# One store of the tail, cut differently: two and a half chunks on 124 and 4 partitions in place of one chunk on 94 and 34

## The chip, the cores and the metric

The kernel runs on one core of one Trainium2 chip. The metric is the device time of one execution in microseconds. The five engines are TensorE (PE, with its weight loads shown as PEld), VectorE (DVE), ScalarE (ACT), GpSimd (POOL) and SyncE (SP). Transfers between HBM and SBUF run on 16 DMA engines that the core's queues share. A transfer that POOL issues is in queue q0 of the profile, one that ACT issues in q10, one that SP issues in q1; q8 and q14 are the queues that bring instructions.

## What is computed

Two stages. The first is cross-covariance attention over channels for four batches, the second a mixture of low-rank adapters on its result, for 25,600 rows of 256 columns:

```python
qn = q / (norm(q, axis=1) + 1e-06); kn = k / (norm(k, axis=1) + 1e-06)   # (4, 6400, 256)
a  = softmax(kn.transpose(0, 2, 1) @ qn / tau)                           # 256 x 256 a batch
x  = (v @ a).reshape(25600, 256)
logits = x @ w_gate                       # 8 experts, the two best are taken
w  = softmax over the two best
out = x + sum over the two of  w * (x @ A[e]) @ B[e]       # rank 16, float32 out
```

The output is 25,600 x 256 float32, 26.2 MB, and the three inputs are as large.

## The kernel before

A batch has 6,400 rows. Partition p holds rows 50p to 50p + 49 of the batch, so a batch is 50 chunks of 128 rows by 256 columns, and a chunk is one row of 1 KB (float32) on each of 128 partitions. Two chunks are a pair; the four batches have 100 pairs, 25 each. In HBM the rows of one partition lie behind each other, so that a store of n chunks is one contiguous run of n KB for each partition.

Loads of q, k and v go through POOL's queue, which casts them to bf16. PE accumulates the 256 x 256 product of a batch (L346), its column norms come from squares (L322, L331), then a short chain makes the softmax. For v, PE transposes the chunks (L507), computes the expert products (L639, L655) and the result of a pair (L672, L681) in PSUM, and ACT or DVE copies it to a staging tile `ys` (L691, L694). A planner in the kernel's Python simulates the engines and writes the order of all instructions out by hand; there is no other scheduler.

Stores. `BLOCKS` (L67) groups the pairs: eight blocks of ten pairs, then blocks of 5 + 5 and of 5 + 4 + 1. Each block has one `ys` tile, of which there are four (`YB`, L52). `send()` (L704) stores one group when all its pairs are in `ys`. Its queue is chosen in L718: POOL's for pairs 0 to 79 (`POOLED`), ACT's for the groups at 80, 85 and 90, SP's for the last two (pairs 95 to 98 and pair 99). A group that is named in `NARROW` (L63), here only that of pairs 80 to 84, is split: nine of its ten chunks go through ACT's queue over all 128 partitions (L722), and the tenth chunk goes through SP's queue as two transfers, partitions 0 to 93 and partitions 94 to 127 (L724). After these two, SP issues only the last two stores (L726) and then waits for all stores to land. The `ys` tile of pairs 80 to 89 is not used again, so no later instruction but the end of the kernel waits for these stores.

Of the kernel before, what the change touches and what calls it, by code (L numbers as in the profile page):

```python
# [16 lines left out]
def kernel(  # L17
# [16 lines left out]
    nc = tc.nc  # L34
    B, N, C = q.shape
    P = 128
# [25 lines left out]
    SPQ = 100  # L62
    NARROW = [80]  # L63
    CONST_SP = 0
    POOLED = range(0, 80)
    SEND_AT = [20, 34, 43, 56, 63]
    BLOCKS = [[10], [10], [10], [10], [10], [10], [10], [10], [5, 5], [5, 4, 1]]  # L67
# [23 lines left out]
    def run(e, us, *deps):  # L91
        clock[e] = max([clock[e]] + [d + (0.0 if e == "pe" else 0.05) for d in deps]) + us
        return clock[e] + (0.2 if e == "pe" else 0.0)
# [3 lines left out]
    def transfer(kind, us, start):  # L97
        x = {"left": us, "start": start, "done": None}
        wire[kind].append(x)
        return x  # L100
# [17 lines left out]
    def backlog():  # L118
        return sum(x["left"] for w in wire.values() for x in w)
# [128 lines left out]
    for n, (tile, src, us) in enumerate(consts):  # L248
        if n < CONST_SP:
            nc.sync.dma_start(tile, src)  # L250
        else:
            nc.gpsimd.dma_start(tile, src)
        transfer("load", us, run("pool", 0.55 if n >= CONST_SP else 0.0) + 1.5)

# [422 lines left out]
    def delta(p):  # L677
        r, x = unit_of[p]
        gr, y = stores[p], pr[p]["y"]
        for sc in range(2):  # L680
            nc.tensor.matmul(y[:, sc, :], r["gzT"][:, 2 * x + sc, :], ball_sb, start=False,  # L681
                             stop=(sc == 1), skip_group_check=True)
        blk = gr["blk"]
        if "ys" not in blk:
            blk["ys"] = y_pool.tile([P, 2 * YG, C], FP32, tag="ys", name="ys")
            ys_used.append(blk)
        w = 2 * (p - blk["f"])
        dst = blk["ys"][:, w:w + 2, :]
        t_end = run("pe", 0.215)
        if clock["dve"] + 1.0 < clock["act"]:  # L690
            nc.vector.tensor_copy(dst, y)  # L691
            end = run("dve", 0.69, t_end)
        else:
            nc.scalar.copy(dst, y)  # L694
            end = run("act", 0.58, t_end)
        pr[p]["y_end"] = gr["y_end"] = end
        if p == gr["f"] + gr["n"] - 1:
            unsent.append(gr)
            if p >= LATE:
                send()  # L700
# [3 lines left out]
    def send():  # L704

        gr = unsent.pop(0)
        f, n, w = gr["f"], 2 * gr["n"], 2 * (gr["f"] - gr["blk"]["f"])
        b, c = f // NPAIR, 2 * (f % NPAIR)
        src = gr["blk"]["ys"][:, w:w + n, :]
        if c + n <= NC:  # L710
            dst = out_v[b, :, c:c + n, :]
        else:

            h = n // 2
            assert c + h == NC
            dst = bass.AP(out.tensor, (b * N + c) * C, [[NC * C, P], [(N - c) * C, 2], [1, h * C]])
            src = src.rearrange("p (x c) d -> p x (c d)", x=2)
        eng = nc.sync if f >= NPT - GRP or f >= SPQ else nc.gpsimd if f in POOLED else nc.scalar  # L718
        if f in NARROW:

            m = n - 1
            eng.dma_start(dst[:, 0:m, :], src[:, 0:m, :])  # L722
            for lo, hi in ((0, 94), (94, P)):
                nc.sync.dma_start(dst[lo:hi, m:n, :], src[lo:hi, m:n, :])  # L724
        else:
            eng.dma_start(dst, src)  # L726
        if eng is nc.gpsimd:
            gr["sent"] = transfer("load", n * CHUNK + 0.05, run("pool", 0.55, gr["y_end"]) + 1.5)
        else:
            gr["sent"] = transfer("store", n * CHUNK + 0.05, run("act", 0.06 if eng is nc.scalar else 0.0, gr["y_end"]) + 3.0)  # L730
# [21 lines left out]
    def last_v():  # L752
        return there("v", B - 1, NC - 1)

    while nd < NPT:
# [5 lines left out]

        while unsent and ((nd >= SEND_AT[unsent[0]["f"] // 10] if unsent[0]["f"] in POOLED and unsent[0]["f"] < 50 else backlog() < BACKLOG) or not loads and not wire["load"] and now > last_v() + 0.0 or
                          sum("sent" not in b["all"][-1] for b in ys_used) > YB - 1):
            send()
# [4 lines left out]
        n = 4 if starved else 1  # L769
# [51 lines left out]
        if nt < NU:  # L821
            r = units[nt]
            ok = nt < VTB or ny >= units[nt - VTB]["p"] + units[nt - VTB]["n"]
            p = r["p"] % NPAIR
# [10 lines left out]
        if gi["b"] < B:  # L835
            b, c = gi["b"], gi["c"]
# [65 lines left out]
    while unsent:  # L902
        send()
# [35 lines left out]
```

## Time and profile before

| | |
|---|---|
| median of 3 runs | 253.91 us (253.84 to 253.92) |
| profiled execution, its own time | 253.94 us |
| span of its trace | 252.1 us |
| outside the span | 1.8 us |
| PE busy | 209.5 us (83%) |
| ACT busy | 167.1 us (66%) |
| DVE busy | 164.6 us (65%) |
| mean busy share of the DMA engines, last 33 us of the span | see the stretches in the prediction |

The page and the views give shares of the 16 DMA engines together. A share of 1.00 means that all 16 work, 0.50 that eight do. A packet is booked with its whole duration to the stretch in which it starts, and successive packets of an engine overlap a little, so that shares can come out slightly above 1. A packet of a store is one contiguous run of one partition; each DMA engine closes its part of a transfer with a 4-byte packet, which the views count among those "under 512 B". The counts "under 2 KB" and "under 8 KB" include the smaller ones. None of the views names the DMA engine of a packet.

### The profile page before, as it was taken

What the parts mean: (1) busy time and instruction counts of PE and PEld (TensorE: products, weight loads), DVE (VectorE), ACT (ScalarE), POOL (GpSimd) and SP (SyncE); (2) the same over time, 40 slices, a digit from 0 to 9 for tenths busy, and PEclk for the clock granted to TensorE, in tenths of its full rate; (3) what the DMA queues carried; (4) which work ended last, traced back from release to release, by engine and by line L of the source; (5) the groups of instructions that cost most, each with busy time, mean ns of one, the idle gap of its engine ahead of it and who ended that gap; (6) DMA issues with size and microseconds to landing.
All of it is one profiled execution on the core that took longest, in us unless ns stands there. A gap on an engine that the chain in (4) does not pass through costs nothing.

```text
span 252.1 us, 6727 instructions
## 1 busy us (share of the span) xinstructions
PE 209.5 (83%) x2870; PEld 185.5 (74%) x2870; DVE 164.6 (65%) x420; ACT 167.1 (66%) x256; POOL 31.0 (12%) x63
## 2 busy tenths in 40 slices
PE   0468088579799999999998999898999999999930
PEld 0345067457688999999997888797988898999820
DVE  1541646774478788887957689769587696777410
ACT  2654065773659678999656598956698768576730
POOL 8111102102201200111301101030020000010000
PEclk9995759968979999999999999999999999999995
DMA  7999999999999999999999999999999999999995
GB/s 219 213 214 214 236 220 214 213 214 213 214 217 220 214 215 217 211 216 218 214 404 235 217 213 219 256 413 383 222 213 222 257 376 310 422 431 412 424 428 209
DMA packets 8898, 66.76 MB, mean 265 GB/s; under 512 B 980, under 2 KB 1124, under 8 KB 5412
## 3 DMA queue, kind: packets, MB, share of 16 engines
q0 software_dynamic: 7872, 60.04, 94.2%
q10 hardware_dynamic: 432, 3.80, 3.6%
q1 hardware_dynamic: 564, 2.49, 2.6%
q8 instruction: 22, 0.36, 0.5%
q14 instruction: 8, 0.07, 0.1%
HBM read 78.91 MB, written 26.21 MB: 417 GB/s over the span
## 4 chain that ended last, share of the span: by engine, by line
DMA 41%; PE 40%; issue 5%; DVE 5%; ACT 2%; POOL 2%; POOLq 0%; DVEq 0%
DMA vt<-in_v_dram 13%; PE y_ps L672 11%; DMA qt<-in_q_dram 10%; DMA kt<-in_k_dram 10%; DMA wst<-in_moe_w_gate_dram 9%; PE acc L346 9%; PE y_ps L681 5%; PE vT_ps L507 5%; PE zg L639 4%; PE zg L655 2%; PE nrm L361 2%; DVE s L331 2%; PE lp L535 1%; ACT sq L322 1%; ACT ys L694 1%
## 5 line engine op out<-in xcount | busy, mean ns | idle before, releaser
L346 PE MATMUL acc<-qt,kt 128*128 128x256 bf16 x400 | 61.2, 309 | 3.9 <-DMA kt<-in_k_dram 3.8
L694 ACT COPY ys<-y_ps 128x512 f32<-128x512 f32 x92 | 52.1, 586 | 15.9 <-PE y_ps L681 14.7
L672 PE MATMUL y_ps<-a_bf,vT 128*128 128x256 bf16 x400 | 59.1, 272 | 1.6 <-ACT ys L694 1.5
L346 PEld LDWEIGHTS <-kt 128*128 128x128 bf16 x400 | 41.9, 110 | 13.2 <-DMA kt<-in_k_dram 4.5
L322 ACT ACTIVATE sq<-qt 128x1024 bf16<-128x1024 bf16 (+1 forms) x42 | 40.6, 1013 | 15.3 <-DVE s L331 13.0
L322 ACT ACTIVATE sq<-kt 128x1024 bf16<-128x1024 bf16 (+1 forms) x43 | 42.2, 1013 | 12.8 <-DVE s L331 7.6
L331 DVE TENSOR_TENSOR s<-sq 128x512 bf16<-128x512 bf16 x104 | 38.6, 408 | 9.1 <-PE nrm L361 5.9
L672 PEld LDWEIGHTS <-vT 128*128 128x128 bf16 x400 | 36.2, 98 | 5.5 <-issue 2.3
L643 DVE TENSOR_TENSOR gz<-zg,e 128x512 bf16<-128x512 f32 (+1 forms) x52 | 33.9, 665 | 9.4 <-PE zg L639 9.1
L361 PE MATMUL nrm<-ones_bf,s 128*128 128x1 bf16 x398 | 21.1, 165 | 21.8 <-DVE s L331 19.8
L361 PEld LDWEIGHTS <-s 128*128 128x128 bf16 x398 | 18.6, 98 | 25.8 <-DVE s L331 22.8
L681 PE MATMUL y_ps<-ball_sb,gzT 128*128 128x256 bf16 x200 | 36.2, 272 | 0.1
L507 PE MATMUL vT_ps<-ident,vt 128*128 128x128 bf16 x400 | 29.9, 219 | 2.2 <-DMA vt<-in_v_dram 1.0
L517 DVE COPY vT<-vT_ps 128x1024 bf16<-128x1024 bf16 (+1 forms) x36 | 23.5, 658 | 12.2 <-PE vT_ps L507 11.8
L639 PE MATMUL zg<-wa_sb,vT 128*128 128x128 bf16 x400 | 29.5, 219 | 0.0
L507 PEld LDWEIGHTS <-vt 128*128 128x128 bf16 x400 | 24.9, 98 | 3.8 <-issue 1.5
L639 PEld LDWEIGHTS <-vT 128*128 128x128 bf16 x400 | 25.1, 98 | 0.5
L514 ACT COPY vT<-vT_ps 128x1024 bf16<-128x1024 bf16 x16 | 16.1, 1014 | 11.7 <-PE vT_ps L507 11.7
L209 POOL DMA_DIRECT2D qt<-in_q_dram x16 | 8.6, 538 | 96.2 <-ACT sq L322 34.1
L655 PE MATMUL zg<-ident,gz 128*128 128x128 bf16 x200 | 19.3, 219 | 0.5 <-DVE gz L643 0.5
L663 DVE COPY gzT<-zg 128x512 bf16<-128x512 bf16 (+1 forms) x33 | 13.3, 408 | 9.1 <-PE zg L655 9.0
L681 PEld LDWEIGHTS <-gzT 128*128 128x128 bf16 x200 | 17.5, 97 | 2.3 <-DVE gzT L663 0.3
(71 smaller groups left out, 169.5 us busy)
## 6 DMA issues: line engine op xcount, KB each, us to landing
out_dram<-ys POOLq DMA_DIRECT2D x8, 2560.0 KB, 36.3
qt<-in_q_dram POOLq DMA_DIRECT2D x12, 768.0 KB, 22.3
kt<-in_k_dram POOLq DMA_DIRECT2D x12, 768.0 KB, 25.4
vt<-in_v_dram POOLq DMA_DIRECT2D x8, 1024.0 KB, 29.9
vt<-in_v_dram POOLq DMA_DIRECT2D x4, 1152.0 KB, 27.0
kt<-in_k_dram POOLq DMA_DIRECT2D x4, 896.0 KB, 22.1
qt<-in_q_dram POOLq DMA_DIRECT2D x3, 896.0 KB, 20.1
out_dram<-ys ACTq DMA_DIRECT2D x2, 1280.0 KB, 11.6
```

Source lines behind the costliest of these rows:

```text
L322: nc.scalar.activation(sq, x, ACT.Square)
L331: nc.vector.tensor_tensor(out=s2, in0=sq[:, 0:n, :], in1=sq[:, n:2 * n, :], op=OP.add)
L346: nc.tensor.matmul(acc[b][:, ic, :], tk[:, o, ic * P:(ic + 1) * P], tq[:, o, :], start=(c == 0 and ic == 0), stop=(c == NC - 1), skip_grou ...
L361: nc.tensor.matmul(nrm[b][:, j:j + 1], s2[:, x, ic * P:(ic + 1) * P], ones_bf[:, 0:1], start=(i == 0 and x == 0 and ic == 0), stop=(i >= l ...
L507: nc.tensor.matmul(pt[:, ic, sc, :], vt[:, o, ic * P:(ic + 1) * P], ident, is_transpose=True, start=(i == 0), stop=(i == 2 * nch - 1))
L517: nc.vector.tensor_copy(vT, pt)
L639: nc.tensor.matmul(z[:, sc, :], r["vT"][:, ic, sc, :], st[b]["wa"][:, ic, E:E + ER], start=(sc == 0 and ic == 0), stop=(sc == nch - 1 and ...
L643: nc.vector.tensor_tensor(out=gz.rearrange("p c (e r) -> p c e r", e=E), in0=z.rearrange("p c (e r) -> p c e r", e=E), in1=gr["gate"][:, r ...
L655: nc.tensor.matmul(gt[:, sc, :], r["gz"][:, sc, :], ident, is_transpose=True, start=(sc == 0), stop=(sc == nch - 1))
L672: nc.tensor.matmul(y[:, sc, :], r["vT"][:, ic, 2 * x + sc, :], st[r["b"]]["a"][:, ic, :], start=(sc == 0 and ic == 0), stop=False, skip_gr ...
L681: nc.tensor.matmul(y[:, sc, :], r["gzT"][:, 2 * x + sc, :], ball_sb, start=False, stop=(sc == 1), skip_group_check=True)
L694: nc.scalar.copy(dst, y)
```

## The change

The group of pairs 80 to 84 is cut at another place. Before, the last of its ten chunks (256 columns, 1 KB a partition) went through SP, cut into 94 and 34 partitions. After, the chunks of a partition are taken as one row of 2,560 columns, of which the last 640 (two and a half chunks, 2.5 KB a partition) go through SP, cut into 124 and 4 partitions. The part that ACT's queue stores over 128 partitions shrinks from nine chunks (9 KB a partition) to seven and a half (7.5 KB). The number of transfers, their queues and their order among the other instructions of each engine stay as they were.

```diff
     SPQ = 100
     NARROW = [80]
     CONST_SP = 0
+    NCOL = 640
+    NROW = 124
...
         if f in NARROW:
 
-            m = n - 1
-            eng.dma_start(dst[:, 0:m, :], src[:, 0:m, :])
-            for lo, hi in ((0, 94), (94, P)):
-                nc.sync.dma_start(dst[lo:hi, m:n, :], src[lo:hi, m:n, :])
+            dst, src = dst.rearrange("p c d -> p (c d)"), src.rearrange("p c d -> p (c d)")
+            m = n * C - NCOL
+            eng.dma_start(dst[:, 0:m], src[:, 0:m])
+            for lo, hi in ((0, NROW), (NROW, P)):
+                nc.sync.dma_start(dst[lo:hi, m:], src[lo:hi, m:])
         else:
             eng.dma_start(dst, src)
```

## The prediction

> **What bounds the kernel now.** I read the last stretches first, because the change touches only a store that is issued at 228 us. Columns: stretch, its length, busy time of PE, PEld, DVE, ACT and POOL with instruction counts, granted clock, share of the 16 DMA engines, GB/s.
>
> ```profile
> 240.00:244.00 4.00, 2.00 (x19) 1.35 (x16) 0.72 (x3) 1.75 (x3) 0.00 (x0) 1.00 1.01 424
> 244.00:248.00 4.00, 0.00 (x0) 0.00 (x0) 0.00 (x0) 0.00 (x0) 0.00 (x0) 0.81 0.92 385
> 248.00:250.80 2.80, 0.00 (x0) 0.00 (x0) 0.00 (x0) 0.00 (x0) 0.00 (x0) 0.50 0.49 200
> 250.80:252.10 1.30, 0.00 (x0) 0.00 (x0) 0.00 (x0) 0.00 (x0) 0.00 (x0) 0.50 0.00 0
> ```
>
> From 244 us on no engine computes; the kernel only drains stores, and the last packet ends at 250.8. The drain is uneven: a share of 0.92, then 0.49. The idle part is 0.08 x 4 x 16 + 0.51 x 2.8 x 16 = 28 engine-us, so a perfectly even drain would end 28 / 16 = 1.75 us earlier. That is the most that any recutting of stores can win.
>
> Next, who drains when. The last store (pair 99) gives every DMA engine eight packets of 2 KB (256 KB over 128 partitions), as the last of its list. Their number is "under 8 KB" minus "under 2 KB", in 240 to 247.0, 247 to 248, 248 to 249.2 and 249.2 to 250.9 us:
>
> ```profile
> DMA packets 441, 2.91 MB, mean 415 GB/s; under 512 B 47, under 2 KB 126, under 8 KB 158
> ...
> DMA packets 48, 0.33 MB, mean 333 GB/s; under 512 B 1, under 2 KB 12, under 8 KB 12
> ...
> DMA packets 77, 0.36 MB, mean 299 GB/s; under 512 B 12, under 2 KB 12, under 8 KB 42
> ...
> DMA packets 93, 0.20 MB, mean 118 GB/s; under 512 B 19, under 2 KB 19, under 8 KB 85
> ```
>
> That is 32, 0, 30 and 66 packets: four engines are through by 247.0, none ends in the next microsecond, between three and four end by 249.2, and some eight to nine between 249.2 and 250.8.
>
> Where the narrow chunk is, in the views of 220 to 253 us, 231.8 to 243.4 us and 232 to 247.46 us:
>
> ```profile
> q1 hardware_dynamic: 420, 1.44, 10.7%
> ...
> DMA packets 599, 4.90 MB, mean 422 GB/s; under 512 B 46, under 2 KB 115, under 8 KB 115
> q10 hardware_dynamic: 311, 2.80, 57.3%
> q1 hardware_dynamic: 69, 0.07, 1.7%
> ...
> DMA packets 870, 6.45 MB, mean 417 GB/s; under 512 B 72, under 2 KB 200, under 8 KB 232
> ```
>
> SP's 420 packets are 128 of 1 KB, 128 of 8 KB, 128 of 2 KB and 36 closing ones. The two full stores close on 16 engines each, which leaves 36 - 32 = 4 for the two narrow ones: two engines each. Of 94 and 34 the only divisors up to 16 are 1 and 2, while 128 has 16, so a transfer seems to use as many engines as divide its partitions. I take both narrow transfers to sit on the same two engines: 47 + 17 = 64 packets of 1 KB on each. By 247.46 us all 128 (200 - 72) have started, the last after 247.4. Behind it the same queue of that engine still holds eight packets of 8 KB and eight of 2 KB, 0.082 MB. The view of 247.46 to 250.8 us gives their price:
>
> ```profile
> q1 hardware_dynamic: 174, 0.63, 46.2%
> ```
>
> 0.462 x 16 x 3.34 us for 0.63 MB is 39 us a MB, so 3.2 us: the later narrow engine ends near 250.65, a hair before the slowest engine at 250.8.
>
> **The change, part by part.** Durations of one packet. 1 KB: 0.017 x 16 x 11.6 us / 69 = 46 ns. 9 KB: q10 in the same view, 0.573 x 16 x 11.6 us / 2.80 MB = 38 us a MB, so 350 ns, and 292 ns for 7.5 KB. 2 KB from the view of 250.4 to 250.9 us, where only the last store runs:
>
> ```profile
> DMA packets 13, 0.02 MB, mean 41 GB/s; under 512 B 3, under 2 KB 3, under 8 KB 13
> q1 hardware_dynamic: 13, 0.02, 10.8%
> ```
>
> 0.108 x 16 x 0.5 us over ten packets is 86 ns. The trace has no packet of 2.5 KB. From below its bytes at 38 us a MB are 97 ns, from above two and a half packets of 1 KB are 115 ns; a line through 46 and 86 ns gives 106 ns, and I take 100, nearer to the long packets, because the bookings overlap (shares of 1.01).
>
> Which engines: 124 and 4 partitions have 4 as their largest common divisor with 16, so by the pattern above each of the new transfers uses four engines, 31 + 1 = 32 packets each. No view shows which; I take the old two to be among them, as the transfers come from the same queue and as a count that does not fill 16 is likely dealt from the same start. The Trainium skill, "DMA: Bandwidth & Descriptors", section "Why a DMA increments its semaphore by 16 and not by 1", says the same of the count and adds that SP's and ACT's transfers take the lowest-numbered engines; the counts of 36 and 420 agree with the first part, no row here can show the second. By it, too, the old two are among the four.
>
> - All 16 engines: eight packets of 7.5 KB in place of 9 KB, 8 x (350 - 292) = 0.47 us less.
> - The two engines that had 1 KB packets: 32 x 100 - 64 x 46 = +0.26 us, less 0.47, so -0.2 us; with the ends 97 and 115 ns it is -0.3 to +0.3.
> - Two engines that had none: 32 x 100 = 3.2 us (3.1 to 3.7) less 0.47, so +2.7 us (2.6 to 3.2).
> - Issue. The three instructions stay where they are:
>
> ```profile
> 228.07 1.37 SPq L724 DMA_DIRECT2D out_dram<-ys  x2
> 229.22 0.38 ACTq L722 DMA_DIRECT2D out_dram<-ys  x1
> 241.75 1.48 SPq L726 DMA_DIRECT2D out_dram<-ys  x2
> SPq L934 <- DMA out_dram<-ys: 7.6, 6, 3.1
> ```
>
> If SP's two took 1.3 times as long (124 partitions against 94), SP would still be free 12 us before its next store at 241.75, and only the end waits for them; cost 0. Without that cover it would be the 0.4 us. ACT's issue stays one instruction; cost 0.
>
> The order of the queues does not matter: each engine has work without a gap to its end, so its end moves by the change of its own sum.
>
> **The sum.** Everything hangs on where the two new engines stood. If they are two of the four that were through by 247.0, they end at 249.6 to 249.8 and are covered by the others. The slowest engines go from 250.8 to 250.3, the later narrow engine from 250.65 to about 250.5 (250.3 to 250.95). The end is then near 250.55, 0.25 us earlier: 253.94 - 0.25 = 253.7 for the profiled execution, which is 0.03 above the median of the runs, so 253.7 again.
>
> Why the four should be among the early. Take the narrow packets away, 64 x 46 ns = 2.9 us, and the two narrow engines would have ended by 247.8, ahead of the gap in which none ends. So six of 16 engines are early without them, and both narrow ones belong to the six; by chance that happens in 6 x 5 of 16 x 15 cases, 1 in 8. Extra work that only some engines carry, such as the instruction fetches
>
> ```profile
> q8 instruction: 22, 0.36, 0.5%
> ```
>
> (0.005 x 16 x 252 us / 22 = 0.9 us each), is then more likely dealt out in blocks of neighbours, and the two neighbours of spared engines are likelier to be spared than 4 x 3 of 14 x 13.
>
> **The rivals.**
>
> *One of the two new engines is a late one of the middle group* (slower). For it: ten of the other 14 engines were not through by 247.0, and the views name no engine. Three or so end between 248.0 and 249.2. Put +2.7 us on one that ended at 248.7 and it ends at 251.4, on one at 249.2 and it ends at 251.9: 0.6 to 1.1 us after 250.8, so 254.5 to 255.0, most likely 254.5, since a spared neighbour with a little extra work is the likeliest of these. It decides as soon as one new engine ended later than 250.8 - 2.7 = 248.1. Against it: the argument of neighbours.
>
> *A new engine is one of the slowest* (slower). Ended 249.2 to 250.8, it now ends at 251.9 to 253.5: 255.0 to 256.6. For it speaks only their number, eight or nine; against it that the first two engines were both early.
>
> *The cut does not use four engines.* If 124 and 4 partitions spread over all 16, each engine would get eight packets of 2.5 KB, 0.8 us, less 0.47 us: the slowest ends 0.3 us later, the narrow ones much earlier, 254.2. If they stayed on two, these would get 64 x 100 ns and end 3 us later; the divisors speak against both. [...]
>
> **How the numbers follow.** Changes within 0.2%, 0.51 us, are about what a measurement of this kernel cannot tell from none: 253.40 to 254.42. All new engines early: 0.41, at 253.7, with its bounds 253.4 to 254.0 (0.03 of it below 253.40, as the relief of the slowest engines by 0.47 us is nearly all that could be won). A middle one: 0.33, at 254.5 to 255.0, of which 0.05 falls inside. A slowest one: 0.18. Spread over 16, or stayed on two: 0.08, nearly all of it the former and inside. So faster 0.03, same 0.38 + 0.05 + 0.08 = 0.51, slower 0.28 + 0.18 = 0.46. The range goes from 253.3 to 255.0 and leaves out the 0.18. The likeliest case alone has 253.4 to 254.0.
>
> **What would show it.** In the profile after, SP's queue has 424 packets in place of 420 (36 + 4 closing ones) if four engines are used, 448 if 16. The last 2 KB packets tell the rest: in the likeliest case 16 of them are written by 247.0 in place of 32, as two of the four early engines are left, and the last is written by 250.6. If the end comes after 251.2 with a share of one engine (0.06) for half a microsecond or more before it, one new engine was late; with two engines (0.12) beyond 252, a slow pair. If the wide part did not shrink each engine's list by 0.47 us, the step with 7.5 KB is wrong; if the packets of 2.5 KB take over 115 ns, the narrow engines set the end.

## The result, and the profile after

The changed kernel takes 254.59 us (median of 10 runs, 254.46 to 254.65), the kernel before 253.91 us (median of 10, 253.83 to 253.98): 0.68 us more, a ratio of 1.0027 with an interval of 1.0017 to 1.0036. The forecast was 253.7; what came is the first rival, a new engine out of the middle group, which was priced at 254.5.

The profiled execution took 254.47 us, with a span of 252.7 us. Its last stretches, in the columns of the stretches before (DMA share and GB/s at the end of the row):

```profile
240.00:244.00 4.00, 2.34 (x23) 1.64 (x20) 1.06 (x3) 1.97 (x4) 0.00 (x0) 1.00 1.00 421
244.00:248.00 4.00, 0.00 (x0) 0.00 (x0) 0.00 (x0) 0.00 (x0) 0.00 (x0) 0.78 0.92 383
248.00:250.80 2.80, 0.00 (x0) 0.00 (x0) 0.00 (x0) 0.00 (x0) 0.00 (x0) 0.50 0.50 205
250.80:251.50 0.70, 0.00 (x0) 0.00 (x0) 0.00 (x0) 0.00 (x0) 0.00 (x0) 0.50 0.06 23
251.50:252.70 1.20, 0.00 (x0) 0.00 (x0) 0.00 (x0) 0.00 (x0) 0.00 (x0) 0.50 0.00 0
```

The DMA shares of the first three rows are those of before within 0.01. The fourth is new: a share of 0.06 for 0.7 us is one engine of 16 (1 / 16 = 0.0625), writing alone where before nothing was written. This is the sign that the prediction named for one late new engine.

The packets of the same execution, in 240 to 247.0, 247 to 248, 248 to 249.2, 249.2 to 250.9 and 250.9 to 251.5 us, and SP's queue in 220 to 254 us:

```profile
DMA packets 397, 2.90 MB, mean 414 GB/s; under 512 B 43, under 2 KB 43, under 8 KB 122
...
DMA packets 50, 0.32 MB, mean 321 GB/s; under 512 B 8, under 2 KB 8, under 8 KB 14
...
DMA packets 88, 0.38 MB, mean 314 GB/s; under 512 B 13, under 2 KB 13, under 8 KB 52
...
DMA packets 87, 0.20 MB, mean 118 GB/s; under 512 B 16, under 2 KB 16, under 8 KB 78
...
DMA packets 7, 0.01 MB, mean 20 GB/s; under 512 B 1, under 2 KB 1, under 8 KB 7
...
q1 hardware_dynamic: 424, 1.64, 11.8%
```

SP's packets went from 420 to 424, so the two new transfers close on four engines each. "Under 8 KB" minus "under 2 KB" now counts packets of 2.5 KB and of 2 KB together: 79, 6, 39, 62 and 6. The records give 64 of the 128 packets of 2.5 KB before 240 and nine after 247.0, so that 55 of the 79 are of 2.5 KB, and 79 - 55 = 24 of the 2 KB packets were written by 247.0: three engines were through, where before there were four and where the likeliest case had two. The last row is the late engine: six packets of 2 KB and their closing packet.

The computation also ended 0.35 us later in this execution. The last copy of ACT, before and then after:

```profile
242.03 0.58 ACT ys L694
```

```profile
242.38 0.59 ACT ys L696
```

That could explain half of the loss, if the last stores were late for all engines. The 15 other engines say no: from 250.9 us on none of them works, and before none worked after 250.8. And in the runs below this copy comes earlier or later without the time following it: at 241.73 us with five engines, 1.72 us slower than before, and at 242.68 us with 384 columns, which is not slower.

**The end of each engine.** No view names the engine of a packet, but the records carry a packet's queue, size, start and duration, and on an engine the next packet begins where the last one ended. So they can be strung into 16 lists. This is a reconstruction, and single links may be wrong; the ends, where few engines are left, are safe. The last packet of each list, in us of the span:

```
kernel   engines with narrow packets         the early ones left     all others end by
before   249.44, 250.57                      4: 246.54 to 246.91     250.80
after    249.35, 249.67, 250.82, 251.46      3: 246.22 to 246.66     250.21
```

In before, the other ten end at 248.68, 249.12, 249.19 and, seven of them, from 250.05 to 250.80. I call the engines by the order in which narrow transfers of two, three, four or five engines reach them: first and second (those of before), third, fourth, fifth. The third is one of the four early ones. The fourth ended at 248.68 before and at 251.46 after, 2.78 us later; the end of the trace moved with it (251.46 - 250.80 = 0.66 us, of 0.68 us in the time).

### The profile page after: what moved, and what is told of

It reads as the page before. It is cut to its first block, busy times and chain, and to the rows that moved or that the text cites. A ratio compares the mean times of both kernels' runs of the same rounds, so it can differ in the third digit from the quotient of the medians.

```text
span 252.7 us, 6727 instructions
## 1 busy us (share of the span) xinstructions
PE 209.3 (83%) x2870; PEld 185.5 (73%) x2870; DVE 164.8 (65%) x420; ACT 167.1 (66%) x256; POOL 31.0 (12%) x63
## 4 chain that ended last, share of the span: by engine, by line
DMA 43%; PE 39%; issue 5%; DVE 5%; ACT 2%; POOL 2%; DVEq 0%; POOLq 0%
DMA vt<-in_v_dram 14%; PE y_ps L674 10%; DMA qt<-in_q_dram 10%; DMA kt<-in_k_dram 10%; PE acc L348 9%; DMA wst<-in_moe_w_gate_dram 9%; PE y_ps L683 5%; PE zg L641 4%; PE vT_ps L509 4%; PE zg L657 2%; PE lp L537 2%; DVE s L333 1%; ACT sq L324 1%; PE nrm L363 1%; ACT ys L696 1%
## 5 line engine op out<-in xcount | busy, mean ns | idle before, releaser
L519 DVE COPY vT<-vT_ps 128x1024 bf16<-128x1024 bf16 (+1 forms) x36 | 23.6, 660 | 12.4 <-PE vT_ps L509 11.8
```

The costliest lines, as they stand in the source:

```text
L519: nc.vector.tensor_copy(vT, pt)
```

## The experiments

The theory was that the time is set by the last engine, and that each engine's end moves by the packets it gains less what the wide store sheds; the third engine would be early and the fourth middle. The rivals in the expectations put the loss down to the larger narrow packets, the number of engines in a narrow transfer, or the later computation. The edits are against the kernel after. Each run has the kernel before on the same chip beside it: 253.72 us for 64 and 64 partitions, 256 columns, three transfers and seven engines; 253.91 for three engines in two transfers, five engines and the first try with memsets; 253.86 for 384 columns and the second try.

**The same bytes on all 16 engines.** The 640 columns are cut into 64 and 64 partitions.

```diff
-            for lo, hi in ((0, NROW), (NROW, P)):
+            for lo, hi in ((0, 64), (64, 128)):
```

> The same 640 columns through SP's queue, but cut into 64 and 64 partitions, which both use all 16 DMA engines: nothing is piled on a few engines any more. Theory T (after the change one of the four engines, a middle one that ended near 248.7 us before, got 3.2 us more and ends last): every engine has 8 x 7.5 KB and 8 x 2.5 KB in place of 8 x 9 KB, +0.33 us against a kernel before whose slowest engines end at 250.8, so 254.2 to 254.3; six engines are through by 247.5 (48 packets of 2 KB). Rival P (packets of 2.5 KB cost far more than 100 ns): as slow as the changed kernel or slower, 254.6 and above. Rival C (the computation ends later with the change, the drain only follows): 254.6, last ACT copy later than 242.0.

253.95 us, 0.23 more than before, ratio 1.001 (1.0 to 1.0019). SP's queue and the last stretches:

```profile
q1 hardware_dynamic: 448, 1.64, 11.1%
...
248.00:250.80 2.80, 0.00 (x0) 0.00 (x0) 0.00 (x0) 0.00 (x0) 0.00 (x0) 0.50 0.47 193
250.80:251.50 0.70, 0.00 (x0) 0.00 (x0) 0.00 (x0) 0.00 (x0) 0.00 (x0) 0.50 0.02 9
```

448 is 64 closing packets, 32 of them for the two narrow transfers: 16 engines each. Bytes, columns, packet size and wide store are those of after, only the engines differ, and 0.45 of the 0.68 us is gone. What is left is the difference of eight packets of 2.5 KB (102 ns each in the records) against 8 x 57 ns from the wide packets, +0.36 us on every engine; the last one ends at 251.05, 0.25 us later than before.

**Four engines, a small piece.** The cut at 124 stays, the piece is one chunk.

```diff
-    NCOL = 640
+    NCOL = 256
```

> The cut at 124 and 4 partitions alone, with the 256 columns of the kernel before: four engines get 32 packets of 1 KB (1.36 us) in place of 64 on two. Theory T: the middle engine ends near 248.7 + 1.36 = 250.05, the slowest engines keep their 250.8, so 253.9 as before. Rival F (four engines as such are slow, through the issue of 124 rows or the third and fourth engine's rate): over 254.2.

253.61 us, 0.11 less, ratio 0.9995 (0.9985 to 1.0004): no change that can be told. The same four engines do no harm by themselves. The fourth now gets 32 packets of 46 ns, which would put it at 248.68 + 1.47 = 250.15; its list ends at 250.01.

**Four engines, one and a half chunks.**

```diff
-    NCOL = 640
+    NCOL = 384
```

> 124 and 4 partitions by 384 columns, between the 256 and the 640 tried. Theory T: 32 packets of 1.5 KB are 1.95 us, so the fourth engine ends at 248.65 - 0.15 + 1.95 = 250.45, the slowest at 250.65: 0.1 to 0.2 us faster than the kernel before. If the loss grew with the width in proportion (from -0.11 at 256 to +0.68 at 640 columns): 0.15 us slower.

253.69 us, 0.17 less, ratio 0.9994 (0.9985 to 1.0002). SP's issue of the last two stores and the last stretches:

```profile
242.40 1.69 SPq L729 DMA_DIRECT2D out_dram<-ys  x2
...
248.00:250.80 2.80, 0.00 (x0) 0.00 (x0) 0.00 (x0) 0.00 (x0) 0.00 (x0) 0.50 0.50 203
250.80:251.50 0.70, 0.00 (x0) 0.00 (x0) 0.00 (x0) 0.00 (x0) 0.00 (x0) 0.50 0.00 0
```

The last stores are issued at 242.40 us, 0.3 us later than in the kernel after (242.10 us, below), and the row of one engine alone has gone. The fourth engine ends at 250.66, by now just the last (the next is at 250.57), but still ahead of the 250.80 of before; somewhere between 384 and 640 columns it begins to cost time. Its step of 0.80 us from 250.66 to 251.46 is that between the two profiled executions (253.66 and 254.47 us); the medians, on two chips, are 0.90 us apart. Against before, the last packet ends 0.14 us earlier, of the 0.17 us in the time.

**Three engines, in three transfers.** 123, 3 and 2 partitions, 432 columns, so that each of three engines gets about as much time as each of four did.

```diff
-    NCOL = 640
+    NCOL = 432
...
-            for lo, hi in ((0, NROW), (NROW, P)):
+            for lo, hi in ((0, 123), (123, 126), (126, 128)):
```

> 123, 3 and 2 partitions by 432 columns: by divisors three engines with 42 packets of 1.7 KB (68 ns each, 2.9 us), one more on the first two. It tells whether the late engine is the third or the fourth. If the fourth: the narrow engines end near 250.6, the slowest at 250.8 - 0.21 = 250.6, so 253.7. If the third: it ends at 248.7 - 0.2 + 2.85 = 251.3, so 254.4 to 254.5. If the transfers don't go by divisors, SP's queue has more than 128 x 3 + 39 = 423 packets of the last 33 us.

254.02 us, 0.30 more, ratio 1.0019 (1.0009 to 1.0028). Neither number. The last packet ends at 250.46, 0.34 us earlier than before, as the theory wants, but the execution takes 252.2 - 250.46 = 1.7 us to its end. What SP waits for at its closing line, in this kernel, and then the head of its page:

```profile
SPq L937 <- DMA out_dram<-ys: 7.5, 2, 7.2
```

```profile
span 252.2 us, 6729 instructions
```

Before, the same wait had six parts with 3.1 us as the longest; now one part of 7.2 us takes nearly all. SP checks its semaphores one after another, and here it stood at that of the last store first. Seven checks followed once the store had landed. The times of these events in the trace, in us:

```
before     250.302  250.615  251.243
k3_432     250.873  250.934  250.999  251.060  251.119  251.181  251.240  251.302
```

Seven steps of 61 ns are 0.43 us. The third narrow transfer is the ninth that SP and ACT issue through their queues, and I read the new order as a semaphore used twice; the order is shown, that cause is argued.

**Three engines, in two transfers.** The same columns, cut into 123 and 5 partitions. The 5 go one each to five engines.

```diff
-    NCOL = 640
-    NROW = 124
+    NCOL = 432
+    NROW = 123
```

> As the cut for three engines with 432 columns, but with two transfers (123 and 5 partitions) in place of three. In the run with three transfers the last packet ended 0.34 us earlier than in the kernel before, yet the time was 0.3 us longer: SP's closing sequence then checked the last store's semaphore first and seven others after it, 62 ns each. Theory T (third engine early, fourth late): without that the gain shows, 0.1 to 0.25 us faster than the kernel before. Rival (three engines are no better balanced and the time follows the number of engines): 0.2 to 0.3 us slower, as with three transfers.

253.72 us, 0.19 less, ratio 0.9993 (0.9984 to 1.0003).

```profile
SPq L937 <- DMA out_dram<-ys: 6.3, 4, 3.6
```

The wait is in four parts again, and the 0.49 us to the run before agree with the 0.43. This is the run that places the engines: three get 42 packets of 72 ns, +2.8 us after the wide store's relief, as much as each of four in the kernel after (32 x 103 ns - 0.46 = 2.8), and nothing is lost. So the third engine was early, and the loss of the kernel after is that of the fourth.

**Five engines.** 544 columns on 125 and 3 partitions: 25 packets of 88 ns on each of five engines.

```diff
-    NCOL = 640
-    NROW = 124
+    NCOL = 544
+    NROW = 125
```

> 125 and 3 partitions by 544 columns: five engines with 25 packets of 2.1 KB (2.1 us), 26 on the first three; every engine is relieved by 0.34 us. It places the fifth engine. Early: the middle engine ends at 248.6 - 0.34 + 2.1 = 250.4, the slowest at 250.45, so 0.3 us faster than the kernel before. Slow (249.7 to 250.8 before): it ends at 251.5 to 252.6, so 0.7 to 1.8 us slower.

255.63 us, 1.72 more, ratio 1.007 (1.0056 to 1.0083).

```profile
248.00:250.80 2.80, 0.00 (x0) 0.00 (x0) 0.00 (x0) 0.00 (x0) 0.00 (x0) 0.50 0.46 186
250.80:251.50 0.70, 0.00 (x0) 0.00 (x0) 0.00 (x0) 0.00 (x0) 0.00 (x0) 0.50 0.06 23
251.50:253.70 2.20, 0.00 (x0) 0.00 (x0) 0.00 (x0) 0.00 (x0) 0.00 (x0) 0.50 0.03 11
```

Again one engine alone (0.06), now until 252.50. Each of the five gains 25 x 88 ns less 8 x 42 ns, 1.87 us, so this one stood at 250.63 without it: one of the slowest seven. Another of the five ends at 250.38, near the 248.68 + 1.87 = 250.55 of the fourth. The fifth engine is the second rival of the prediction, met one engine later.

**Seven engines.** 800 columns, 119, 7 and 2 partitions.

```diff
-    NCOL = 640
+    NCOL = 800
...
-            for lo, hi in ((0, NROW), (NROW, P)):
+            for lo, hi in ((0, 119), (119, 126), (126, 128)):
```

> 119, 7 and 2 partitions by 800 columns: by divisors seven engines with 18 packets of 3.1 KB (2.2 us), 19 on the first two. Theory T with the early engines as neighbours (all three that are early in both traces are the fifth to seventh): the slowest engines go from 250.8 to 250.15, the middle one to 248.7 - 0.65 + 2.2 = 250.25, so 253.3 to 253.4, faster than both. If one of the fifth to seventh is a slow engine it ends near 252.3, so 255.4 or so.

255.71 us, 1.99 more, ratio 1.0079 (1.0062 to 1.0095).

```profile
q1 hardware_dynamic: 432, 1.72, 11.7%
```

432 packets are 16 closing ones for the narrow transfers, 7 + 7 + 2. The last packet ends at 252.14, 1.34 us later than before; SP's seven checks behind the last store are there again (252.613 to 253.042 us), and with their 0.43 us that is 1.77 of the 1.99 us. Engines in a block of neighbours are not spared alike.

**What makes the fourth engine later, first try.** Both kernels, before and after, get 400 short memsets of DVE spread over the first stage, so that DVE fetches more instructions.

```diff
+    spare = const.tile([P, 2], BF16)
...
+        for _ in range(2):
+            nc.vector.memset(spare, 0.0)
```

> The kernel before with 400 more memsets of two columns on DVE, two ahead of each step of the 256 x 256 products; they change nothing that is stored. Theory I (the late engine is late since it brings DVE's instructions, four fetches of 8 KB at about 0.5 us each): three more fetches make that engine 1.5 us later, near 250.2, still ahead of 250.8; so the time is that of the kernel before but for what 24 us more of DVE work cost (0 to 0.5 us). Rival L (it is late for its place): the same.

> The changed kernel with the same 400 memsets. Theory I: its late engine ends 1.5 us later still, so it is 1.8 to 2.3 us slower than the kernel before with the memsets, where without them the difference was 0.68 us. Rival L: the difference stays at 0.6 to 0.7 us.

269.05 us for before and 268.82 us for after (1.06 and 1.0569). The memsets of the first kernel, with their busy time, mean duration and the idle time ahead of them:

```profile
L344 DVE MEMSET spare<- 128x1 uint32 x400 | 23.6, 59 | 20.0
```

23.6 us of busy time and 20.0 us of idle time sit in the first stage, where the norms wait for DVE (PE's waits for L331 go from 19.8 to 32.5 us). At most 0.5 us was expected of the memsets; they cost 15. The computation ends so late (the last copy of ACT at 262.1 us, the last packet at 265.6) that it hides the drain. Inconclusive.

**Second try.** 110 memsets of DVE behind the last send, for one fetch more at the end.

```diff
+    spare = const.tile([P, 2], BF16)
+    for _ in range(110):
+        nc.vector.memset(spare, 0.0)
```

> The kernel before with 110 memsets of two columns on DVE behind its last work (60 ns each, 6.6 us from 241.6 on, so done by 248.5, ahead of the drain's end); they change nothing that is stored, but make DVE bring one more block of 8 KB. Theories I and L alike: that block falls on an engine with 2 us to spare, so no change within 0.1 us.

> The changed kernel with the same 110 memsets. Theory I (its late engine is the one that brings DVE's instructions, 0.3 to 0.5 us a block): 0.3 to 0.5 us slower than the changed kernel, so 1.0 to 1.2 us slower than the kernel before. Rival L (the engine is late for its place, DVE's blocks come on another): 0.6 to 0.7 us slower than the kernel before, as without them.

258.40 us and 258.59 us (1.0173 and 1.018). What SP waits for at the end of the first of them:

```profile
SPq L937 <- DVE spare L906: 5.9, 1, 5.9
SPq L937 <- DMA out_dram<-ys: 5.0, 3, 2.9
```

DVE itself, which ran 13.7 us on these memsets where 6.6 were expected, is waited for in place of the stores. The times are inconclusive too: both tries changed more than the fetch. But the traces say where the added fetch went. The queue q14, which has eight packets of 8 KB in both kernels, has nine here and eleven in the first try, so it brings DVE's instructions. In the changed kernel the ninth starts at 251.448 us, just as the late engine's closing packet ends (251.443 to 251.452), which places it on that engine; in the kernel before it starts at 249.891. Behind the engine's last store it could not make the stores later.

## Why the prediction was wrong, point by point

- *The kernel is bound by the drain of the stores, and by the last engine of it.* Right. In after, with 16 engines, with five and with seven, the last packet moved by +0.66, +0.25, +1.70 and +1.34 us, the time by +0.68, +0.23, +1.72 and, with the 0.43 us of its third transfer, +1.99.
- *Four engines.* Right: 424 packets. The counts of the other cuts (448 for 64 and 64, 432 for 119, 7 and 2) follow the rule of the largest divisor up to 16, and the Trainium skill, "DMA: Bandwidth & Descriptors", section "Why a DMA increments its semaphore by 16 and not by 1", which states it, agrees. The largest common divisor with 16, as the prediction also put it, gives the same for 124 and 4, but 1 for 119 and for 7, where 432 shows seven. The Trainium skill's order, the lowest-numbered engines, fits so far as the lists go: each larger cut kept the engines of the smaller one. No view shows an engine's number.
- *The durations.* Right. A packet of 2.5 KB took 103 ns in the records (priced at 100), one of 7.5 KB 295 ns (292). A new engine's +2.7 us came out as the fourth's 2.78, and the later of the two old narrow engines ended at 250.82, inside the stated 250.3 to 250.95.
- *Issue and waits.* Right. The instructions stood where they were expected, SP was free long before its next store:

```profile
228.41 1.51 SPq L727 DMA_DIRECT2D out_dram<-ys  x2
242.10 1.71 SPq L729 DMA_DIRECT2D out_dram<-ys  x2
```

- *The two new engines are early ones.* This is the step that failed: "Everything hangs on where the two new engines stood", and "the two neighbours of spared engines are likelier to be spared". One of the two neighbours was (the third), one was not (the fourth, 248.68), and the next was among the slowest (the fifth). That two neighbours were both early was taken as a sign of blocks; with 248.68 the fourth had passed the point of 248.1 us from which the prediction's own rival decides. That rival named 248.7 as the likeliest place and 251.4 as the new end; measured 248.68 and 251.46.
- *Why is the fourth late?* Part of the answer can be read, none was shown by a change. In the reconstructed lists the fourth engine carries four of the eight fetches of 8 KB, at 37, 91, 156 and 211 us, and is some 0.5 us later behind each, 2.1 us in all: about the distance from the early engines (246.5 to 246.9) to 248.68. Of the other four fetches of 8 KB, one is on the third engine and three are on one of the first two, which ends at 250.57 where its twin with none ends at 249.44. The fetches of 16 KB go in turn over eight other engines, none of the first five: the two that carry two of them end at 249.12 and 249.19, the six that carry three are among the slowest seven. The profile has the two queues as:

```profile
q8 instruction: 22, 0.36, 0.5%
q14 instruction: 8, 0.07, 0.1%
```

So the fetches fit the order in which 15 of the 16 engines end. Among the first four, taken as neighbours, they are dealt out 0 and 3 (the first two, in either order), 1 and 4, and not alike as the prediction thought likely. The ninth fetch above agrees that DVE's fall on the fourth engine. Where the fourth would end without them no run shows. The fifth engine carries no fetch at all; its list shows some 70 packets stretched by 20 to 180 ns, at 129 to 132, 164 to 175 and from 202 us on, 3.8 us in all, in the kernel before as well. What stretches them stays open.

The two versions that the runs point to, 384 columns on four engines and 432 on three in two transfers, are 0.17 and 0.19 us faster than before in the median, but both intervals hold 1.

## What to carry to other kernels

Where a kernel ends in a drain of stores, its end is the end of the slowest DMA engine; the mean share of the 16 says how much could be won, not which engine has room. Before piling a piece on few engines, place them: a run with a small piece on k engines costs nothing here, and the lists of packets then give the end of each engine and so the largest piece that fits. Spare engines that lie side by side are not equally spare.

## What was not expected of the hardware

- The number of transfers has a price at the end, apart from their bytes: with three narrow transfers, in both runs that had them, SP's last seven checks came after the last store, 61 ns each, 0.43 us.
- Engines that carry equal shares of all stores ended 4.3 us apart (246.5 to 250.8 us) in a kernel of 254 us, and on all three chips of the experiments the fourth ended 1.6 to 2.3 us behind the two earliest engines with narrow packets (runs with 256 and 384 columns and with five engines).
